# K of cache A two heads to a load, two K slots and two V slots, softmax and PV by head pair

## The chip, the cores and the metric

The kernel runs on one core of a Trainium2 chip. The core has a matrix engine (PE, with its weight loads shown as PEld), a vector engine (DVE), an activation engine (ACT), GpSimd (POOL) and SyncE (SP), which here issues nearly all loads. 16 DMA engines move the data between device memory and the core's own memory (SBUF, 128 partitions). The metric is the time of one execution on the device in microseconds (us).

## The reference

Two decode attentions stand side by side, A and B, each with its own inputs. Both have 32 query heads, 32 key and value heads of 16384 positions and 128 columns, and one query position. A attends to all positions, B to the last 4096.

```python
q = (x @ wq).reshape(B, Sq, Hq, Dh)              # x: 1 x 1 x 512, wq: 512 x 4096, bf16
k = k_cache ; v = v_cache                        # A: all 16384 positions
k = k_cache[:, :, Sk - W:, :]                    # B: W = 4096, v likewise
scores = jnp.einsum("bhqd,bhkd->bhqk", q, k) * (Dh ** -0.5)
p = _softmax(scores, axis=-1)
o = jnp.einsum("bhqk,bhkd->bhqd", p, v)
out = o.reshape(B, Sq, Hq * Dh) @ wo             # wo: 4096 x 512
return jnp.concatenate([a, b], axis=-1)
```

K and V are read once: 32 heads of 4 MiB each for A's K and for A's V, and as much as 8 heads each for B's.

## The kernel before

**Tiles.** The work is cut into 40 tiles of 4 MiB of K and 4 MiB of V (list `tiles`, L83). A tile of A is one head: each of the 128 partitions holds 128 consecutive positions, a row of 32 KB. A tile of B is four heads: partition 4i + h holds 128 positions of the window of head h. After every first of four A tiles stands a B tile.

**Buffers.** One ring of five slots of 32 KB per partition (`slot`, L62) holds K tiles, V tiles, the two wq and the two wo. Slots are handed out in the order of the loads: wq of A, K(0), wq of B, K(1), then V(t-1) and K(t+1) in turn. At the end come wo of B, V(38), V(39) and wo of A, the last in five pieces of 16, 8, 4, 2 and 2 rows (`wo_pieces`). All of these go through SP's queue, which works in order: a load whose slot isn't free holds up those behind it.

**One tile.** DVE multiplies K by the query row (`scores_prod`, L160), adds halves of the columns four times (`scores_tree`, L169), reduces the last eight columns (L173) and takes the maximum of each partition (`tile_max`, L180). PE transposes these maxima into one row (L182), DVE takes the maximum of the row (`max_all`, L187), one for A, four for B, which are spread to a row of 128 by a copy `Mr` (L194), and PE sends it back to all partitions (L198). ACT makes the bias (L207) and the exponentials with their sum (`soft`, L210); PE adds the sums over the partitions (L216). For B, ACT multiplies the exponentials by four masks into `pm` (L220), so that a matmul keeps four heads apart. PV is 32 matmuls of 128 x 512 (`pv`, L240), DVE inverts the sum (`recip`, L229), ACT scales the result (`evict`, L249), and four small matmuls turn it into a column of the output (`columns`, L259).

**Order.** The program is written out by hand (`manual_schedule`). In iteration t, DVE multiplies tile t before it takes the row maximum of tile t-1, then does the tree of tile t. PE's PV of tile t-1 runs beside that tree.

**End.** The last two tiles of A use V as weights and give a column directly (`pv_column`, L269). `permute_o` (L276 to L284) reorders the heads, `project_out_columns` (L294) multiplies by wo and `store_out` writes 512 columns. B's output is stored during the last iteration, A's last, as the pieces of its wo land.

Of the kernel before, what the change touches and what calls it, by code (L numbers as in the profile page):

```python
# [9 lines left out]
F32 = mybir.dt.float32  # L10
BF16 = mybir.dt.bfloat16
P = 128
# [5 lines left out]
NB = 5  # L18
# [8 lines left out]
def kernel(  # L27
# [22 lines left out]
    NI = P // 4  # L50
    assert WB == NI * CH

    singles = ctx.enter_context(tc.tile_pool(name="singles", bufs=1))
    ring = ctx.enter_context(tc.tile_pool(name="ring", bufs=NB))
    small = ctx.enter_context(tc.tile_pool(name="small", bufs=3))
    o_pool = ctx.enter_context(tc.tile_pool(name="o4", bufs=2))
# [5 lines left out]
    def slot(name):  # L62
        return ring.tile([P, CH, DH], BF16, tag="ring", name=name)
# [4 lines left out]
    ones_col = singles.tile([P, 1], F32, tag="ones_col")  # L68

    A, B = _Side(), _Side()  # L70
    for s, n, x, wq, wo in ((A, "A", A_x, A_wq, A_wo), (B, "B", B_x, B_wq, B_wo)):
        s.n, s.x, s.wq, s.wo = n, x, wq, wo
        s.xT = singles.tile([P, KC], BF16, tag=f"xT{n}", name=f"xT{n}")
        s.nh = 1 if n == "A" else 4
        s.xb = singles.tile([P, s.nh, KC, P], BF16, tag=f"xb{n}", name=f"xb{n}")
        s.q = singles.tile([P, HQ // s.nh, DH], BF16, tag=f"q{n}", name=f"q{n}")
        s.O = singles.tile([P, HQ], BF16, tag=f"O{n}", name=f"O{n}")
        s.Op = singles.tile([P, HQ], BF16, tag=f"Op{n}", name=f"Op{n}")
    mask4 = singles.tile([P, 4], F32, tag="mask4")
    mask16 = singles.tile([P, 4, 4], F32, tag="mask16")  # L80
    pick = singles.tile([HQ, 4, P], BF16, tag="pick")

    tiles = []  # L83
    for g in range(HQ // 4):
        tiles += [("A", 4 * g), ("B", g), ("A", 4 * g + 1), ("A", 4 * g + 2), ("A", 4 * g + 3)]
    NT = len(tiles)

    def load_kv(dst, cache, t):
        kind, h = tiles[t]
        if kind == "A":  # L90
            nc.sync.dma_start(out=dst[:, :, :], in_=cache[0][0, h, :, :].rearrange("(p l) d -> p l d", p=P))
        else:
            nc.sync.dma_start(
                out=dst[:, :, :].rearrange("p l d -> p (l d)"),
                in_=cache[1][0, 4 * h : 4 * h + 4, SkB - WB : SkB, :].rearrange(
                    "h (i l) d -> i h (l d)", l=CH
                ),
            )

    KSRC, VSRC = (A_k_cache, B_k_cache), (A_v_cache, B_v_cache)  # L100
    K, V = {}, {}

    def load_k(t):
        K[t] = slot("kt")
        load_kv(K[t], KSRC, t)

    def load_v(t):
        V[t] = slot("vt")
        load_kv(V[t], VSRC, t)

    def load_wq(s):
        s.wq_t = slot("wqt")
        nc.sync.dma_start(  # L113
            out=s.wq_t[:, :, :].rearrange("p a b -> p (a b)").rearrange("p (c f) -> p c f", c=KC),
            in_=s.wq.rearrange("(p c) f -> p c f", c=KC),
        )

    def load_wo(s, pieces):
        s.wo_t = slot("wot")
        dst = s.wo_t[:, :, :].rearrange("p a b -> p (a b)").rearrange("p (r f) -> p r f", r=HQ)  # L120
        src = s.wo.rearrange("(p r) f -> p r f", r=HQ)
        r = 0
        for n in pieces:
            nc.sync.dma_start(out=dst[:, r : r + n, :], in_=src[:, r : r + n, :])
            r += n

    def spread_x(s):
        if s.nh == 1:
            nc.vector.tensor_copy(s.xb[:, 0, :, :], s.xT[:, :].unsqueeze(2).broadcast_to([P, KC, P]))
        else:  # L130
            nc.vector.memset(s.xb[:, :, :, :], 0.0)
            for j in range(s.nh):
                nc.vector.tensor_copy(
                    s.xb[:, j, :, :].rearrange("p c (i h) -> p c i h", h=s.nh)[:, :, :, j],
                    s.xT[:, :].unsqueeze(2).broadcast_to([P, KC, P // s.nh]),
                )

    def project_q(s):
# [3 lines left out]
        G = HQ // s.nh  # L142
        for g in range(0, G, 4):
# [10 lines left out]
    sc, pt, mx, sm, osb = {}, {}, {}, {}, {}  # L154

    def scores_prod(t):
        kind, h = tiles[t]
        k = K[t]
        q = (A if kind == "A" else B).q
        nc.vector.tensor_tensor(  # L160
            out=k[:, :, :], in0=k[:, :, :], in1=q[:, h : h + 1, :].broadcast_to([P, CH, DH]), op=ALU.mult
        )

    def scores_tree(t):
        k = K[t]
        sc[t] = small.tile([P, CH], F32, tag="sc", name="sc")
        w = DH // 2
        while w >= 8:
            nc.vector.tensor_tensor(  # L169
                out=k[:, :, 0:w], in0=k[:, :, 0:w], in1=k[:, :, w : 2 * w], op=ALU.add  # L170
            )
            w //= 2
        nc.vector.tensor_reduce(out=sc[t][:, :], in_=k[:, :, 0:8], axis=AX.X, op=ALU.add)  # L173

    def nq_of(t):
        return 1 if tiles[t][0] == "A" else 4

    def tile_max(t):
        m = small.tile([P, 1], F32, tag="m", name="m")
        nc.vector.tensor_reduce(out=m[:, :], in_=sc[t][:, :], axis=AX.X, op=ALU.max)  # L180
        sm[t] = ps_m.tile([P, 512], F32, tag="sm", name="sm")
        nc.tensor.transpose(sm[t][0:1, 0:P], m[:, :], identf[:, :])  # L182

    def max_all(t):
        nq = nq_of(t)
        M = small.tile([1, 4], F32, tag="M", name="M")
        nc.vector.tensor_reduce(  # L187
            out=M[:, 0:nq], in_=sm[t][0:1, 0:P].rearrange("o (i q) -> o q i", q=nq), axis=AX.X, op=ALU.max
        )
        if nq == 1:  # L190
            row = M[:, 0:1].broadcast_to([1, P])
        else:
            Mr = small.tile([1, P], F32, tag="Mr", name="Mr")
            nc.vector.tensor_copy(  # L194
                Mr[:, :].rearrange("o (i q) -> o i q", q=nq), M[:, :].unsqueeze(1).broadcast_to([1, P // nq, nq])
            )
            row = Mr[:, :]
        nc.tensor.matmul(sm[t][:, 128:129], lhsT=row, rhs=one_f[:, :], start=True, stop=True)  # L198

    def rows_of(t):  # L200
        if t >= NT - 2:
            return P
        return 4 if tiles[t][0] == "A" else 16

    def soft(t):
        bias = small.tile([P, 1], F32, tag="bias", name="bias")
        nc.scalar.activation(out=bias[:, :], in_=sm[t][:, 128:129], func=ACT.Copy, scale=-inv)  # L207
        pt[t] = small.tile([P, CH], BF16, tag="p", name="p")
        cs = small.tile([P, 1], F32, tag="cs", name="cs")
        nc.scalar.activation(  # L210
            out=pt[t][:, :], in_=sc[t][:, :], func=ACT.Exp, scale=inv, bias=bias[:, :], accum_out=cs[:, :]
        )
        ns = rows_of(t)
        lhsT = cs[:, :].broadcast_to([P, ns]) if ns != 16 else mask16[:, :, :].rearrange("p a b -> p (a b)")
        rhs = ones_col[:, :] if ns != 16 else cs[:, :]
        nc.tensor.matmul(sm[t][0:ns, 136:137], lhsT=lhsT, rhs=rhs, start=True, stop=True)  # L216
        if ns == 16:
            pm = o_pool.tile([P, CH // 4, 4, 4], BF16, tag="pm", name="pm")
            for j in range(4):
                nc.scalar.activation(  # L220
                    out=pm[:, :, j, :], in_=pt[t][:, :].rearrange("p (i c) -> p i c", c=4),
                    func=ACT.Copy, scale=mask4[:, j : j + 1],
                )
            pt[t] = pm

    def recip(t):
        ns = rows_of(t)
        r = small.tile([P, 1], F32, tag="r", name="r")
        nc.vector.reciprocal(r[0:ns, :], sm[t][0:ns, 136:137])  # L229
        sm[t, "r"] = r  # L230

    def pv(t):
        n = rows_of(t)
        o = ps_o.tile([16, 512], F32, tag="o", name="o")
        for i in range(CH // 4):
            if n == 4:
                lhsT = pt[t][:, 4 * i : 4 * i + 4]
            else:
                lhsT = pt[t][:, i, :, :].rearrange("p a b -> p (a b)")
            nc.tensor.matmul(  # L240
                o[0:n, :], lhsT=lhsT, rhs=V[t][:, 4 * i : 4 * i + 4, :],
                start=(i == 0), stop=(i == CH // 4 - 1),
            )
        sm[t, "o"] = o

    def evict(t):
        n = rows_of(t)
        osb[t] = o_pool.tile([16, 512], F32, tag="o4", name="o4")
        nc.scalar.activation(  # L249
            out=osb[t][0:n, :], in_=sm[t, "o"][0:n, :], func=ACT.Copy, scale=sm[t, "r"][0:n, 0:1]  # L250
        )

    def columns(t):
        kind, h = tiles[t]
        n, nq = rows_of(t), nq_of(t)
        oc = sm[t][:, 140 : 140 + nq]
        sel = identf[0:n, 0:n].rearrange("k (h c) -> k c h", c=4)
        for j in range(4):
            nc.tensor.matmul(  # L259
                oc, lhsT=osb[t][0:n, j * P : (j + 1) * P], rhs=sel[:, j, :], start=(j == 0), stop=(j == 3)  # L260
            )
        s = A if kind == "A" else B
# [153 lines left out]
```

## Time and profile before

| | |
|---|---|
| time, median of 3 runs (lowest to highest) | 829.92 us (829.76 to 830.18) |
| the profiled execution: its own time | 830.12 us |
| its span in the profile | 828.3 us |
| mean clock granted to PE | 0.72 of full |
| read from device memory | 352.32 MB, mean 426 GB/s of traffic |
| busy: DVE, PE, PEld, ACT | 764.5, 461.9, 203.9, 77.8 us |
| a K load, a V load, from issue to landing (median) | 38.6, 29.7 us |

How to read the profile: engines are shown with the time in which an instruction ran on them. A group of instructions is named by its line (L160 is line 160 of the kernel), its engine and operation, and the tiles that it writes and reads. `out<-in 128x512 bf16` gives partitions, elements and type; `x32` is a count. In the timeline a row begins with the start and the duration in us, and in brackets stands the idle time before it, with what ended it. In the list of waits a row gives the waiting engine, what it waited for, the total in us, how often and the longest. The page's slices are 40 equal parts of the span. The DMA queue q1 is SP's.

### The profile page before, as it was taken

How to read it: one execution, taken by the hardware profiler on the slowest of the kernel's cores; microseconds unless marked ns; L12 is line 12 of the kernel's file. 1: busy time of each engine (PE TensorE's matmuls, PEld its weight loads, DVE VectorE, ACT ScalarE, POOL GpSimd, SP SyncE). 2: the span in 40 equal slices, each digit the busy share in tenths (PEclk: the TensorE clock that was granted, in tenths of full speed). 3: DMA queues.
4: the chain of work that ended last, by engine and by line, in shares of the span. 5: the costliest groups of instructions: out<-in, count | busy, mean ns of one | idle time of the engine just before them, and what ended most of it. 6: DMA issues, size and time to landing. Idle time of an engine off the chain costs nothing.

```text
span 828.3 us, 5565 instructions
## 1 busy us (share of the span) xinstructions
PE 461.9 (56%) x2308; PEld 203.9 (25%) x2308; DVE 764.5 (92%) x387; ACT 77.8 (9%) x247; POOL 0.7 (0%) x6
## 2 busy tenths in 40 slices
PE   3544655555555656556655555555565565555645
PEld 1212222222222222222222222222222222222234
DVE  1899999999999999999999999999999999999980
ACT  1101100010001100010100100001100100011110
POOL 0000000000000000000000000000000000000000
PEclk9776876776776677777777677666667787776755
DMA  9999999999999999999999999999999999999996
GB/s 380 430 430 430 430 430 430 435 435 434 431 432 432 428 434 432 428 430 431 432 430 430 432 430 434 432 428 432 429 434 432 432 430 434 430 430 435 431 430 260
DMA packets 13000, 352.68 MB, mean 426 GB/s; under 512 B 1712, under 2 KB 1712, under 8 KB 2096
## 3 DMA queue, kind: packets, MB, share of 16 engines
q1 hardware_dynamic: 12680, 352.33, 99.0%
q8 instruction: 18, 0.29, 0.1%
q10 hardware_dynamic: 296, 0.00, 0.0%
q14 instruction: 6, 0.05, 0.0%
HBM read 352.32 MB, written 0.00 MB: 425 GB/s over the span
## 4 chain that ended last, share of the span: by engine, by line
DMA 68%; DVE 18%; PE 12%; ACT 1%; issue 0%; SPq 0%; DVEq 0%
DMA kt<-in_A_k_cache_dram 47%; DMA kt<-in_B_k_cache_dram 14%; DVE kt L160 14%; PE o L240 11%; DMA wot<-in_A_wo_dram 4%; DMA wot<-in_B_wo_dram 4%; DVE kt L169 3%; PE sm L198 1%; ACT p L210 1%; DVE sc L173 0%; ACT pm L220 0%; DVE M L187 0%; ACT bias L207 0%; PE sm L216 0%; SPq L113 0%
## 5 line engine op out<-in xcount | busy, mean ns | idle before, releaser
L169 DVE TENSOR_TENSOR kt<-kt 128x8192 bf16<-128x8192 bf16 (+3 forms) x160 | 344.5, 2153 | 4.2
L160 DVE TENSOR_TENSOR kt<-kt,qA 128x16384 bf16<-128x16384 bf16 x32 | 278.2, 8693 | 14.3 <-DMA kt<-in_A_k_cache_dram 13.8
L240 PE MATMUL o<-vt,p 128*4 128x512 bf16 x960 | 276.7, 460 | 0.6 <-DMA vt<-in_A_v_cache_dram 0.6
L240 PEld LDWEIGHTS <-p 128*4 128x4 bf16 x960 | 92.7, 98 | 170.1 <-issue 94.2
L198 PE MATMUL sm<-one_f,M 1*128 1x1 f32 x64 | 18.6, 357 | 205.9 <-DVE M L187 205.9
L240 PE MATMUL o<-vt,pm 128*16 128x512 bf16 x256 | 74.2, 462 | 8.8 <-ACT pm L220 8.8
L160 DVE TENSOR_TENSOR kt<-kt,qB 128x16384 bf16<-128x16384 bf16 x8 | 69.5, 8693 | 2.6 <-DMA kt<-in_B_k_cache_dram 2.6
L198 PEld LDWEIGHTS sm<-one_f,M 1*128 1x128 f32 x64 | 15.9, 306 | 209.0 <-DVE M L187 209.0
L249 ACT ACTIVATE o<-o,r 4x512 f32<-4x512 f32 (+1 forms) x38 | 25.8, 678 | 356.7 <-PE o L240 330.5
L259 PE MATMUL sm<-identf,o 4*128 4x1 f32 (+1 forms) x304 | 39.8, 248 | 19.1 <-ACT o L249 18.9
L173 DVE TENSOR_REDUCE sc<-kt 128x128 f32<-128x1024 bf16 x40 | 48.8, 1220 | 1.4
L259 PEld LDWEIGHTS sm<-identf,o 4*128 4x128 f32 (+1 forms) x304 | 36.6, 186 | 26.5 <-ACT o L249 26.5
L240 PEld LDWEIGHTS <-pm 128*16 128x16 bf16 x256 | 26.3, 105 | 53.4 <-issue 24.6
L198 PE MATMUL sm<-one_f,Mr 1*128 1x1 f32 x16 | 4.7, 357 | 59.8 <-DVE Mr L194 59.8
L207 ACT ACTIVATE bias<-sm 128x1 f32<-128x1 f32 x40 | 6.9, 172 | 286.7 <-PE sm L198 286.7
L216 PE MATMUL sm<-ones_col,cs 128*4 128x1 f32 (+1 forms) x64 | 6.9, 177 | 25.2 <-ACT p L210 25.2
L198 PEld LDWEIGHTS sm<-one_f,Mr 1*128 1x128 f32 x16 | 4.0, 306 | 60.4 <-DVE Mr L194 60.4
L306 DVE TENSOR_REDUCE cols<-out_cols 128x4 f32<-128x20 f32 x1 | 0.2, 179 | 18.9 <-PE out_cols L294 18.9
L148 PE MATMUL qp<-wqt,xbA 128*128 128x512 bf16 x32 | 9.6, 475 | 13.6 <-DMA wqt<-in_A_wq_dram 13.6
L210 ACT ACTIVATE p<-sc,bias 128x128 bf16<-128x128 f32 x40 | 16.1, 402 | 1.3
L182 PE MATMUL sm<-identf,m 128*1 128x128 f32 x40 | 10.9, 272 | 6.3 <-DVE m L180 6.2
L148 PE MATMUL qp<-wqt,xbB 128*128 128x512 bf16 x32 | 8.4, 428 | 9.9 <-DMA wqt<-in_B_wq_dram 9.9
(54 smaller groups left out, 116.6 us busy)
## 6 DMA issues: line engine op xcount, KB each, us to landing
kt<-in_A_k_cache_dram SPq DMA_DIRECT2D x32, 4096.0 KB, 38.6
vt<-in_A_v_cache_dram SPq DMA_DIRECT2D x32, 4096.0 KB, 29.7
kt<-in_B_k_cache_dram SPq DMA_DIRECT2D x8, 4096.0 KB, 38.7
vt<-in_B_v_cache_dram SPq DMA_DIRECT2D x8, 4096.0 KB, 29.7
wqt<-in_A_wq_dram SPq DMA_DIRECT2D x1, 4096.0 KB, 12.8
wqt<-in_B_wq_dram SPq DMA_DIRECT2D x1, 4096.0 KB
wot<-in_B_wo_dram SPq DMA_DIRECT2D x1, 4096.0 KB, 29.4
wot<-in_A_wo_dram SPq DMA_DIRECT2D x1, 2048.0 KB, 33.5
```

The costliest lines, as they stand in the source:

```text
L148: nc.tensor.matmul(qp[:, :, :], lhsT=s.xb[:, j, c, :], rhs=wq[:, c, j, g : g + 4, :], start=(k == 0), stop=(k == n - 1),)
L160: nc.vector.tensor_tensor(out=k[:, :, :], in0=k[:, :, :], in1=q[:, h : h + 1, :].broadcast_to([P, CH, DH]), op=ALU.mult)
L169: nc.vector.tensor_tensor(out=k[:, :, 0:w], in0=k[:, :, 0:w], in1=k[:, :, w : 2 * w], op=ALU.add)
L173: nc.vector.tensor_reduce(out=sc[t][:, :], in_=k[:, :, 0:8], axis=AX.X, op=ALU.add)
L182: nc.tensor.transpose(sm[t][0:1, 0:P], m[:, :], identf[:, :])
L198: nc.tensor.matmul(sm[t][:, 128:129], lhsT=row, rhs=one_f[:, :], start=True, stop=True)
L207: nc.scalar.activation(out=bias[:, :], in_=sm[t][:, 128:129], func=ACT.Copy, scale=-inv)
L210: nc.scalar.activation(out=pt[t][:, :], in_=sc[t][:, :], func=ACT.Exp, scale=inv, bias=bias[:, :], accum_out=cs[:, :])
L216: nc.tensor.matmul(sm[t][0:ns, 136:137], lhsT=lhsT, rhs=rhs, start=True, stop=True)
L240: nc.tensor.matmul(o[0:n, :], lhsT=lhsT, rhs=V[t][:, 4 * i : 4 * i + 4, :], start=(i == 0), stop=(i == CH // 4 - 1),)
L249: nc.scalar.activation(out=osb[t][0:n, :], in_=sm[t, "o"][0:n, :], func=ACT.Copy, scale=sm[t, "r"][0:n, 0:1])
L259: nc.tensor.matmul(oc, lhsT=osb[t][0:n, j * P : (j + 1) * P], rhs=sel[:, j, :], start=(j == 0), stop=(j == 3))
```

## The change

The loads of A's K take two heads at once: partition 64h + i of an 8 MiB tile holds 256 positions of head h of the pair, a row of 64 KB. There are two slots of 64 KB per partition for K and two of 32 KB for V in place of five of 32 KB. A step T is a pair of tiles: a pair of A's heads, or two B tiles of four heads. V of a step comes in two loads of 4 MiB: for an A pair each takes 128 of the 256 positions of every partition, so it is read in rows of 32 KB that stand 64 KB apart. B's tiles keep their layout. The steps of B are the first, 7, 13 and the last, 19.

DVE's product, tree and reduction run on half a step at a time (u = 0, 1), 4 MiB as before. For an A pair there is one softmax for both heads, over 256 columns per partition, with two masks into `pm`; the sum of PV over both halves goes into one accumulator. For B there is a softmax for every half. PV of an A pair is two times 32 matmuls with 8 rows of output instead of 4: `pv(T-2, 1)` and `pv(T-1, 0)` both stand in the first half of step T. The last half step uses V as weights, for four heads of B; A's output is stored first, B's last, as the pieces of its wo land. The scratch for B's spread x takes a K slot at the start.

SP's order in step T is V(T-1, 0), K(T+1), V(T-1, 1). In step 19 it is V(18, 0), V(18, 1), V(19, 0), wo of A, V(19, 1), wo of B in five pieces.

The core of the diff:

```diff
-    ring = ctx.enter_context(tc.tile_pool(name="ring", bufs=NB))
+    kring = ctx.enter_context(tc.tile_pool(name="kring", bufs=2))
+    vring = ctx.enter_context(tc.tile_pool(name="vring", bufs=2))
...
+    def kslot(name):
+        return kring.tile([P, 2 * CH, DH], BF16, tag="kring", name=name)
+
+    def vslot(name):
+        return vring.tile([P, CH, DH], BF16, tag="vring", name=name)
...
+    for T in range(HQ // 2 + HQ // 8):
+        if T in (0, 7, 13, 19):
+            steps.append((B, nb))
+            nb += 1
+        else:
+            steps.append((A, na))
+            na += 1
...
+    def b_window(cache, g):
+        return cache[0, 4 * g : 4 * g + 4, SkB - WB : SkB, :].rearrange("h (i l) d -> i h (l d)", l=CH)
+
+    def a_pair(cache, g):
+        return cache[0, 2 * g : 2 * g + 2, :, :].rearrange("h (i l) d -> (h i) l d", l=2 * CH)
...
+    def load_k(T, u=None):
+        s, g = steps[T]
+        if s is A:
             nc.sync.dma_start(
...
+                out=K[T][:, :, :].rearrange("p l d -> p (l d)"),
+                in_=a_pair(A_k_cache, g).rearrange("p l d -> p (l d)"),
+            )
+        else:
+            for v in (0, 1) if u is None else (u,):
+                nc.sync.dma_start(
+                    out=K[T][:, v * CH : (v + 1) * CH, :].rearrange("p l d -> p (l d)"),
+                    in_=b_window(B_k_cache, 2 * g + v),
+                )
+
+    def load_v(T, u):
+        s, g = steps[T]
+        V[T, u] = vslot("vt")
+        if s is A:
+            src = a_pair(A_v_cache, g)[:, u * CH : (u + 1) * CH, :].rearrange("p l d -> p (l d)")
+        else:
+            src = b_window(B_v_cache, 2 * g + u)
+        nc.sync.dma_start(out=V[T, u][:, :, :].rearrange("p l d -> p (l d)"), in_=src)
...
+    def unit_max(un):
         m = small.tile([P, 1], F32, tag="m", name="m")
...
+        nc.vector.tensor_reduce(out=m[:, :], in_=un.sc[:, 0 : un.n], axis=AX.X, op=ALU.max)
+        un.sm = ps_m.tile([P, 512], F32, tag="sm", name="sm")
+        nc.tensor.transpose(un.sm[0:1, 0:P], m[:, :], identf[:, :])
...
+        for j in range(s.nh):
+            nc.scalar.activation(
+                out=un.pm[:, :, j, :], in_=p[:, 0 : un.n].rearrange("p (i c) -> p i c", c=4),
+                func=ACT.Copy, scale=s.mask[:, j : j + 1],
+            )
...
+    def pv(T, u):
+        s = steps[T][0]
+        un = units[T, u if s is B else 0]
+        first, final = (True, True) if s is B else (u == 0, u == 1)
+        if first:
+            un.o = ps_o.tile([16, 512], F32, tag="o", name="o")
+        i0 = u * CH // 4 if s is A else 0
+        for i in range(CH // 4):
+            nc.tensor.matmul(
+                un.o[0 : un.rows, :],
+                lhsT=un.pm[:, i0 + i, :, :].rearrange("p a b -> p (a b)"),
+                rhs=V[T, u][:, 4 * i : 4 * i + 4, :],
+                start=(first and i == 0),
+                stop=(final and i == CH // 4 - 1),
             )
...
+        for x in range(2 * NT):
+            T, u = divmod(x, 2)
+            if u == 0 and T >= 1:
+                load_v(T - 1, 0)
+                if T + 1 < NT:
+                    new_k(T + 1)
+                    load_k(T + 1)
+            if x == 2 * NT - 1:
+                load_v(T, 0)
+                W = kslot("wot")
+                load_wo(A, W, 0, (HQ,))
+            columns()
+            scores_prod(T, u)
+            if done is not None:
+                max_all(done)
+                soft(done)
+            if u == 0 and T >= 1:
+                if T >= 2:
+                    pv(T - 2, 1)
+                load_v(T - 1, 1)
+                pv(T - 1, 0)
+            if x == 2 * NT - 1:
+                pv(T - 1, 1)
+                load_v(T, 1)
+                load_wo(B, W, 1, wo_pieces)
+            nxt = scores_tree(T, u)
+            if done is not None:
+                recip(done)
+            evict()
+            done = nxt
+            if done is not None:
+                unit_max(done)
```

## The prediction

> **What bounds the kernel now.** I read the page first, slices and chain before groups, then the waits of all engines and of SP's queue, then the timeline of the last 90 us. From the page:
>
> ```profile
> span 828.3 us, 5565 instructions
> ...
> PE 461.9 (56%) x2308; PEld 203.9 (25%) x2308; DVE 764.5 (92%) x387; ACT 77.8 (9%) x247; POOL 0.7 (0%) x6
> ...
> GB/s 380 430 430 430 430 430 430 435 435 434 431 432 432 428 434 432 428 430 431 432 430 430 432 430 434 432 428 432 429 434 432 432 430 434 430 430 435 431 430 260
> ...
> q1 hardware_dynamic: 12680, 352.33, 99.0%
> ...
> DMA 68%; DVE 18%; PE 12%; ACT 1%; issue 0%; SPq 0%; DVEq 0%
> ```
>
> The DMA engines are 99% occupied and move 428 to 435 GB/s in every slice but the first and the last. The kernel is bound by 84 loads of 4 MiB: at 432 GB/s one takes 4.194/0.432 = 9.71 us, and 84 take 815.6. DVE at 92% is close behind. The waits say how close:
>
> ```profile
> DVE kt L160 <- DMA kt<-in_A_k_cache_dram: 13.8, 25, 3.0
> DVE kt L160 <- DMA kt<-in_B_k_cache_dram: 2.6, 8, 0.4
> ```
>
> DVE waits for K only 16.4 us in 40 tiles. The issuing queue is the third clock:
>
> ```profile
> SPq L91 <- DVE m L180: 544.0, 30, 20.7
> SPq L93 <- DVE m L180: 149.2, 8, 19.2
> ```
>
> SP spends its time waiting for ring slots, yet the median K load lands 38.6 us after its issue (part 6 of the page), four loads' worth: slots come free two loads ahead of need. No idle DMA is visible for a better order to recover. From the timeline:
>
> ```profile
> 745.30 8.69 DVE L160 TENSOR_TENSOR kt<-kt,qA 128x16384 bf16<-128x16384 bf16 x1 [0.39 <-DMA kt<-in_A_k_cache_dram]
> ...
> 754.22 0.21 DVE L194 COPY Mr<-M 1x128 f32<-1x128 f32 x1
> ...
> 757.16 9.89 PE L240 MATMUL o<-vt,pm 128*16 128x512 bf16 x32 [1.09 <-ACT pm L220]
> ...
> 764.74 8.69 DVE L160 TENSOR_TENSOR kt<-kt,qA 128x16384 bf16<-128x16384 bf16 x1
> ...
> 784.09 8.69 DVE L160 TENSOR_TENSOR kt<-kt,qA 128x16384 bf16<-128x16384 bf16 x1 [0.26 <-DMA kt<-in_A_k_cache_dram]
> ```
>
> A step with B's four-row softmax takes 764.74 - 745.30 = 19.44 us of DVE, one with A's 784.09 - 764.74 - 0.26 + 0.1 of usual spacing = 19.19. The wait at 784.09 is for the last K, the 80th load. Loads 81 to 84 and the last wo piece (first used at 824.72) follow 40.6 us behind, and 3.6 us after that the span ends. The time before is 830.12 for this execution (span 828.3) and 829.92 in the median, 0.2 apart, so a difference of ends carries over to the median.
>
> **The change, part by part.**
>
> *Bytes.* The same 84 x 4 MiB. A's K goes in 16 loads of 8 MiB with 64 KB rows. In the trace's DMA records a packet of 32 KB takes 1.215 us and one of 16 KB 0.612, so 16 KB cost 0.603 and a packet about 9 ns more. If 64 KB go as one packet, each of 16 DMA engines saves 8 x 9 ns a pair, 1.15 us in 16 pairs; if rows are cut at 32 KB, nothing. Fewer DMAs save nothing else: landings follow each other at 9.71 us, the packets' own time. *DMA: Bandwidth & Descriptors* (Anatomy of one DMA) in the Trainium skill puts about 2.0 us of fixed cost on a DMA, measured on another issue path; by that, 16 fewer would save up to 32 us.
>
> *Row pitch.* A's V is read as 32 KB rows 64 KB apart, A's K as an unbroken 8 MiB. B's tiles already take neighbouring partitions from heads 4 MiB apart, and their stretches run at the same 429 to 432 GB/s. I take no loss. The same page (Latency and other measured facts) speaks against the change here: row pitches of large powers of two lose rate, 3% at 512 KiB and half at 4 MiB. B's rows contradict it at 4 MiB; by its 3%, 32 V loads would cost 9.3 us.
>
> *DVE.* The product (8.69), tree (8.72) and reduction (1.22) are unchanged per 4 MiB. Per A pair the change takes away one maximum over partitions (0.1 on DVE's path), one reciprocal (0.04) and one row maximum (0.3), adds the Mr copy (0.2 to 0.25), and lengthens the remaining row maximum from 128 to 256 columns (0 to 0.29 more, from 0.286; I take 0.13). A pair is 2 x 19.19 - 0.44 + 0.25 + 0.13 = 38.3; bounds 38.1 to 38.5. A B pair is 2 x 19.44 = 38.9. The loads of a pair take 38.85. So DVE and DMA run nearly level, as before.
>
> *ACT and PE.* Two mask multiplications of 256 columns per pair (0.390 for 128, so about 0.5 each) lie beside DVE's tree. PE's 32 matmuls per 4 MiB of V stay. They come as 64 in a row once per pair: pv(T-2,1), then pv(T-1,0). The trace has no such burst. Alone, 32 take 8.6 to 9.9: the first 13 start 0.427 apart, the rest 0.21. So the first half takes 9.5 and the second between 32 x 0.21 = 6.8 and 9.5; I take 6.8, since the spacing doesn't grow again within a burst. *TensorE: Matmul & The Clock Gate* (Part 1) says the clock doubles after some 3.4 us of activity and falls back after an idle window of that length; the rows show about 5.5 us, and the rule too gives 6.8.
>
> *Queue, in the body.* SP now waits for pv(T-2,1) before it issues V(T-1,1), and V(T,0) and K(T+2) stand behind that wait. From the step's start: product 8.69; maximum and Mr 0.45; broadcast on PE 0.6; bias, exponential over 256 columns, its accumulator and the row-sum matmul 1.15; together 10.9. Then 9.5 of PV: the slot is free at 20.4. Meanwhile V(T-1,0) and the 8 MiB K(T+1) have kept the DMA engines busy for 29.1 us from about the step's start. Covered by 8 us; cost nothing. K(T+1) needs its slot at the step's start and has V(T-1,0)'s 9.7 us as cover. Two B steps (7 and 13) have a maximum whose transpose queues behind both PVs: 10.9 + 9.5 + 6.8 + 0.3 = 27.5, against DVE's arrival at 19.44 + 8.69 = 28.1. No wait at the chosen PV, 2 us each at the slow one.
>
> *Queue, at the end.* In step 19 there is no K(20). V(18,0), the 79th load, is alone in the queue, and V(18,1), the 80th, is not issued until pv(17,1) ends; V(19,0), wo of A, V(19,1) and wo of B stand behind it. The cover of 19.4 us is gone.
>
> - DVE starts at 23.4 as before, since K still lands second. The first B pair ends at 42.8 + 19.44 = 62.3 (42.8 is where DVE starts its second tile now, its load being fourth in both; halves of a slot are waited for apart, as the pieces of wo are now at 822.16 and 823.43). Then 16 x 38.3 + 2 x 38.9 = 690.6: step 19 starts at 752.9 by DVE alone.
> - By DMA: K(18) is loads 72 and 73. Load 76 starts the product of 745.30, so load 73 ends at 745.0 - 29.1 = 715.9, or 714.8 with larger packets. Plus 0.3 and step 18's 38.3: 753.4 to 754.5.
> - Both agree; I take 754.2. Plus 20.4 is 774.6, when SP may issue. The kernel's first load takes from 0.74 to 2.17 from issue to its first byte, 1.4; so 776.1.
> - Load 79 ends at 784.1 - 9.7 = 774.4. The engines idle 1.7 us.
> - Load 80 takes 9.71 plus a restart. The first load landed at 13.62, 1.7 later than 2.17 + 9.71; bounds 0 and 1.7, I take 0.7, nearer zero because three other first loads were issued within the same 2 us there. It is usable at 776.1 + 9.7 + 0.7 + 0.2 = 786.7, against 784.1.
>
> The four loads behind it are as many and as cut as now, and the end is the same chain of projection, transpose and store. pv(18,0) ends at 774.6 + 6.8 = 781.4, before load 80 does, and pv(18,1) at about 796.5, before wo of A (about 806) does, so no second gap. Sum: 786.7 - 784.1 = 2.6 later; 829.9 + 2.6 = 832.5.
>
> **Rivals.**
>
> - *The gap doesn't open.* If DVE's pair is 38.1 and 64 KB packets are real, step 19 starts at 752.5 to 753; with no restart cost load 80 is usable within 1.4 us of its old time. 830.1, from 829.2 to 831.5. For it: the two clocks differ by under 0.2%. Against: it needs the favourable end of three terms.
> - *Slow PV.* If the second PV stays at 9.5, two B steps lose 2 us each, and a first PV up to 10.5 adds 1: 754.2 + 2 to 4 + 20.4 to 21.4. 836, to 838.
> - *DMA slowed by the new rows.* 0.5% of A's K and V, 2/3 of 650 us: 2 to 3 us more than the forecast, 835.
> - *Faster, by quicker K rows.* It decides once load 80 lands before 782.4, so step 19 must start by 749.9 and K(18) land by 711.3, 4.6 earlier than now. Seventeen pairs of K, 330 us, would have to run 1.4% faster, and DVE's pair to take 38.1. The packets explain 1.15 us. 827.5.
> - *It doesn't do what it says:* rows cut into 32 KB packets. That moves the DMA line by 1.1 us and is inside the forecast's range.
>
> **How the numbers follow.** Forecast 0.55, its own range 830.6 to 834.5; no gap 0.21; slow PV 0.11; slower rows 0.07; faster 0.06. No change means within 0.2%, 1.7 us, about what a measurement of this kernel can tell. About 0.06 of the forecast's chance and nearly all of the second case lie there: same 0.26, faster 0.07, slower 0.67. The range from 829.4 to 836.5 leaves out the faster case, the worst of slow PV and small parts of the rest.
>
> **What would show it.** Right: no "9" missing in the DMA slices until a dip around 774; SP's longest late wait ends with PE's PV; the product of step 19 starts near 754; V(18,1) lands near 787; 64 matmuls in a row with 16.3 us between first and last. Wrong: slices of the body above 434 or below 429 GB/s; DVE waiting for the transposed maximum in B steps; waits for K of several us in A steps; a step 19 that starts before 751 or after 757.

## The result, and the profile after

The changed kernel takes 831.33 us in the median of 14 runs (830.11 to 832.50), the kernel before 829.86 in 14 runs beside it (829.58 to 830.18): 1.47 us slower, a ratio of 1.0018 with a 95% interval of 1.0010 to 1.0026. The profiled execution took 831.32, with a span of 829.5.

The page of the changed kernel, lines that answer to those shown of before: span, busy time by engine, what the DMA engines moved in each of 40 slices, SP's queue, and the chain that ended last.

```profile
span 829.5 us, 4817 instructions
...
PE 395.2 (48%) x2012; PEld 172.7 (21%) x2012; DVE 761.0 (92%) x356; ACT 67.8 (8%) x196; POOL 0.7 (0%) x6
...
GB/s 379 430 430 437 433 458 411 453 408 432 435 427 430 437 455 411 450 412 448 416 444 417 440 425 431 450 416 450 416 441 420 444 417 443 425 433 433 331 431 305
...
q1 hardware_dynamic: 10376, 352.33, 98.7%
...
DVE 79%; DMA 17%; PE 2%; issue 1%; SPq 0%; ACT 0%; DVEq 0%; ACTq 0%
```

One slice stands out, the 38th with 331 GB/s (767 to 788 us). The swing of the others around 432 is a matter of counting (see the section on why the prediction was right); the dip is real. The windows around it, first of the changed kernel, then of the one before (stretch, length, busy time of each engine with its instructions, granted clock, DMA share, GB/s):

```profile
760.00:767.00 7.00, 3.94 (x12) 1.54 (x13) 6.93 (x5) 1.68 (x5) 0.00 (x0) 0.50 0.97 417
767.00:774.00 7.00, 7.00 (x30) 2.63 (x29) 6.83 (x7) 0.68 (x1) 0.00 (x0) 0.87 0.45 190
774.00:781.00 7.00, 7.00 (x36) 3.10 (x35) 7.00 (x2) 0.00 (x0) 0.00 (x0) 1.00 0.99 393
```

```profile
767.00:774.00 7.00, 1.64 (x12) 1.36 (x11) 7.00 (x3) 0.84 (x2) 0.00 (x0) 0.70 1.01 435
```

Before, the DMA engines were full in these 7 us; now they are 45% full, so on average each stands idle for 3.9 us. What they wait for stands in SP's own waits between 773 and 774 us and in the timeline of the changed kernel:

```profile
SPq L131 <- PE o L275: 9.9, 1, 9.9
```

```profile
752.99 8.68 DVE L194 TENSOR_TENSOR kt<-kt,qB 128x16384 bf16<-128x16384 bf16 x1
...
763.70 16.50 PE L275 MATMUL o<-vt,pm 128*8 128x512 bf16 x64
...
773.31 0.33 SPq L131 DMA_DIRECT2D vt<-in_A_v_cache_dram  x1
...
785.39 8.98 PE L275 MATMUL o<-vt,pm 128*8 128x512 bf16 x32 [2.48 <-DMA vt<-in_A_v_cache_dram]
...
825.78 0.38 PE L345 MATMUL out_cols<-OpB,wot 128*128 128x1 bf16 x8 [0.27 <-DMA wot<-in_B_wo_dram]
```

Step 19 begins at 752.99; `pv(17, 1)` and `pv(18, 0)` are the 64 matmuls from 763.70; when the first 32 are done, SP issues V(18,1), the 80th load, at 773.31, and PE can use it at 785.39. In the kernel before the 80th load was used at 784.09. From there on both kernels run alike: the last wo piece is used at 825.78 against 824.72, and the span ends 3.7 us later against 3.6.

### The profile page after: what moved, and what is told of

Its sections match the earlier page's. It is cut to its first block, busy times and chain, and to the rows that moved or that the text cites. A ratio compares the mean times of both kernels' runs of the same rounds, so it can differ in the third digit from the quotient of the medians.

```text
span 829.5 us, 4817 instructions
## 1 busy us (share of the span) xinstructions
PE 395.2 (48%) x2012; PEld 172.7 (21%) x2012; DVE 761.0 (92%) x356; ACT 67.8 (8%) x196; POOL 0.7 (0%) x6
## 3 DMA queue, kind: packets, MB, share of 16 engines
q1 hardware_dynamic: 10376, 352.33, 98.7%
## 4 chain that ended last, share of the span: by engine, by line
DVE 79%; DMA 17%; PE 2%; issue 1%; SPq 0%; ACT 0%; DVEq 0%; ACTq 0%
DVE kt L194 36%; DVE kt L201 35%; DMA kt<-in_A_k_cache_dram 10%; DVE sc L207 5%; DMA wot<-in_B_wo_dram 3%; DMA xTA<-in_A_x_dram 3%; PE o L275 2%; DMA vt<-in_A_v_cache_dram 1%; DVE m L212 1%; DVE Mr L223 1%; DVE M L219 0%; SPq L145 0%; DVE r L263 0%; ACT p L234 0%; PE sm L226 0%
## 5 line engine op out<-in xcount | busy, mean ns | idle before, releaser
L275 PE MATMUL o<-vt,pm 128*8 128x512 bf16 (+1 forms) x1248 | 316.3, 420 | 2.5 <-DMA vt<-in_A_v_cache_dram 2.5
L275 PEld LDWEIGHTS <-pm 128*8 128x8 bf16 (+1 forms) x1248 | 116.2, 94 | 192.5 <-issue 65.1
L226 PE MATMUL sm<-one_f,Mr 1*128 1x1 f32 x48 | 13.1, 340 | 176.7 <-DVE Mr L223 176.7
L226 PEld LDWEIGHTS sm<-one_f,Mr 1*128 1x128 f32 x48 | 11.1, 285 | 183.1 <-DVE Mr L223 183.1
L291 ACT ACTIVATE o<-o,r 8x512 f32<-8x512 f32 (+1 forms) x23 | 15.6, 678 | 176.5 <-PE o L275 176.5
L306 PE MATMUL oc<-identf,o 8*128 8x2 f32 (+1 forms) x184 | 25.1, 254 | 3.7 <-ACT o L291 3.7
L306 PEld LDWEIGHTS oc<-identf,o 8*128 8x128 f32 (+1 forms) x184 | 23.1, 193 | 12.0 <-issue 6.5
L172 PE MATMUL qp<-wqt,scratch 128*128 128x512 bf16 x32 | 9.1, 455 | 13.8 <-DVE scratch L161 13.8
L253 ACT ACTIVATE pm<-p,maskA 128x256 bf16<-128x256 bf16 x32 | 14.5, 500 | 0.5
L234 ACT ACTIVATE p<-sc,bias 128x256 bf16<-128x256 f32 (+1 forms) x24 | 11.3, 472 | 0.8
L253 ACT ACTIVATE pm<-p,maskB 128x128 bf16<-128x128 bf16 x32 | 10.2, 389 | 0.2
```

Source lines behind the costliest of these rows:

```text
L172: nc.tensor.matmul(qp[:, :, :], lhsT=s.xb[:, j, c, :], rhs=wq[:, c, j, g : g + 4, :], start=(k == 0), stop=(k == n - 1),)
L226: nc.tensor.matmul(un.sm[:, 128:129], lhsT=Mr[:, :], rhs=one_f[:, :], start=True, stop=True)
L234: nc.scalar.activation(out=p[:, 0 : un.n], in_=un.sc[:, 0 : un.n], func=ACT.Exp, scale=inv, bias=bias[:, :], accum_out=cs[:, :],)
L253: nc.scalar.activation(out=un.pm[:, :, j, :], in_=p[:, 0 : un.n].rearrange("p (i c) -> p i c", c=4), func=ACT.Copy, scale=s.mask[:, j : j ...
L275: nc.tensor.matmul(un.o[0 : un.rows, :], lhsT=un.pm[:, i0 + i, :, :].rearrange("p a b -> p (a b)"), rhs=V[T, u][:, 4 * i : 4 * i + 4, :], ...
L291: nc.scalar.activation(out=un.osb[0 : un.rows, :], in_=un.o[0 : un.rows, :], func=ACT.Copy, scale=un.r[0 : un.rows, 0:1],)
```

## The experiments

Three explanations compete. Theory 1: the end moves with the landing of the 80th load, and this waits for `pv(17, 1)` to free a V slot. Theory 2: the end is set by DVE's step after step, as the chain's 79% suggests. Theory 3: the idle time only lets late DMA engines catch up, so closing it would gain little.

**V(18,1) into a slot that is free (e1_slot).** The K slot of step 18 is empty when step 19 begins. V(18,1) goes there, and the loads behind it are spread over what is left.

```diff
+                else:
+                    W = kslot("wot")
+                    load_v(T - 1, 1, W[:, 0:CH, :])
             if x == 2 * NT - 1:
                 load_v(T, 0)
-                W = kslot("wot")
-                load_wo(A, W, 0, (HQ,))
+                load_wo(A, vslot("wot"), 0, (HQ,))
+                load_v(T, 1, W[:, CH : 2 * CH, :])
...
-                load_v(T, 1)
-                load_wo(B, W, 1, wo_pieces)
+                load_wo(B, W, 0, wo_pieces)
```

> V(18,1) is loaded into the K slot that step 18 has left, so it no longer waits for pv(17,1); V(19,0) and wo of A take the two V slots, V(19,1) and wo of B the halves of that K slot. Theory 1 (the whole loss is the wait before the 80th load): the 80th load follows the 79th without a pause, is usable at about 782.9 instead of 785.4, and the end comes 2.0 to 2.6 us earlier: 828.7 to 829.3, below the kernel before. Theory 2 (DVE's chain of step after step, 79% of the chain that ended last, sets the end): within 0.5 us of 831.3. Theory 3 (the restart only lets lagging DMA engines catch up, so closing it gives the lag back): a gain under 1 us, 830.3 to 831.3.

Measured: 828.14 us (11 runs, 827.75 to 828.96), a ratio of 0.9979 to the kernel before, 0.9970 to 0.9988; 3.2 us below the changed kernel. Its timeline and its window:

```profile
752.51 0.33 SPq L131 DMA_DIRECT2D wot<-in_A_v_cache_dram  x1
...
763.56 8.51 PE L275 MATMUL o<-vt,pm 128*8 128x512 bf16 x32
...
782.72 8.75 PE L275 MATMUL o<-wot,pm 128*8 128x512 bf16 x32
```

```profile
767.00:774.00 7.00, 6.06 (x29) 2.37 (x28) 6.83 (x7) 0.68 (x1) 0.00 (x0) 1.00 1.00 428
```

SP issues the load 20.8 us earlier, the engines stay full, and PE uses the load at 782.72, 2.7 earlier. Step 19 begins when it did (752.86 against 752.99), so DVE's chain up to there is unchanged while the end came 3.2 us earlier: theory 2 is out, and so is theory 3, which allowed less than 1 us. This version beats both kernels.

A part of theory 3 does show at the load itself: the engines had idled 3.9 us each, and the load came only 2.7 earlier. By the landing records of the two traces, the 16 engines finish V(18,1) within 0.5 us of each other after the gap (784.87 to 785.35) and 3.3 us apart without it (779.41 to 782.68), so late engines do catch up in the gap. But nothing is given back in the end: the last piece of wo lands at 821.85 instead of 825.73, the whole 3.9 us earlier.

**A lighter DVE (e5_light).** The other end of theory 2:

```diff
-        while w >= 8:
+        while w >= 16:
```

> The last of the four additions of each tree (8 columns, 0.69 us on DVE) is left out, so the scores lack columns 8 to 15; DVE has 28 us less to do over the run. Theory 1: the loads and then the wait for pv(17,1) set the end; V(17,1) lands at 763.2 whatever DVE does, so pv(17,1) can start at most 0.5 us earlier, and DVE waits for K instead: 830.7 to 831.4. Theory 2 (DVE's chain sets the end): at least 3 us less, 828.3 or below.

Measured: 830.86 us (11 runs), 0.5 below the changed kernel. Its page and its waits:

```profile
DMA 49%; DVE 45%; PE 5%; issue 0%; SPq 0%; ACT 0%; DVEq 0%
```

```profile
DVE kt L194 <- DMA kt<-in_A_k_cache_dram: 23.9, 12, 3.2
DVE kt L194 <- DMA kt<-in_B_k_cache_dram: 5.4, 2, 4.4
```

```profile
763.09 9.12 PE L275 MATMUL o<-vt,pm 128*8 128x512 bf16 x32 [1.05 <-DMA vt<-in_A_v_cache_dram]
...
772.24 0.33 SPq L131 DMA_DIRECT2D vt<-in_A_v_cache_dram  x1
```

DVE is busy for 26.5 us less (734.5 against 761.0), and its waits for K grow by 26.3, from 3.0 to 29.3. The same 80th load is issued at 772.24, after a `pv(17, 1)` that now starts as its V lands. DVE and the DMA engines take nearly the same time for a step (38.1 us a pair in the changed kernel against four loads of 9.7). The chain's 79% DVE had shown only that DVE was the later of the two at most steps; the share didn't tell what a faster DVE brings.

**A's K in two loads of 32 KB rows (e2_rows32).**

```diff
-            nc.sync.dma_start(
-                out=K[T][:, :, :].rearrange("p l d -> p (l d)"),
-                in_=a_pair(A_k_cache, g).rearrange("p l d -> p (l d)"),
-            )
+            for v in (0, 1):
+                nc.sync.dma_start(
+                    out=K[T][:, v * CH : (v + 1) * CH, :].rearrange("p l d -> p (l d)"),
+                    in_=a_pair(A_k_cache, g)[:, v * CH : (v + 1) * CH, :].rearrange("p l d -> p (l d)"),
+                )
```

> A's K is loaded in two halves of 32 KB rows per pair, all else as in the changed kernel. Theory 1: packets of 32 KB only, so each DMA engine needs 1.15 us more over the run; V(17,1) lands about 1.1 later, pv(17,1) starts 0.5 to 1.1 later, and the end moves by as much: 831.8 to 832.5. Theory 2 (DVE's chain): no change or a small gain, since a product can start on half a pair: 830.8 to 831.4. If long rows were bad for the transfers, 830 or less.

Measured: 832.12 us (8 runs, 831.62 to 832.78), 0.8 above the changed kernel. Products could start on half a pair and step 19 began earlier, at 749.95, yet `pv(17, 1)` did not:

```profile
764.85 16.75 PE L276 MATMUL o<-vt,pm 128*8 128x512 bf16 x64 [4.05 <-DMA vt<-in_A_v_cache_dram]
...
774.46 0.33 SPq L132 DMA_DIRECT2D vt<-in_A_v_cache_dram  x1
```

It waits 4.05 us for V(17,1), which lands 1.4 us later by the landing records (764.81 against 763.40). Each DMA engine has two packets of 32 KB in place of one of 64 KB, 128 times, at 10 ns more each time: an estimated 1.3 of it. The 80th load is issued 1.15 later and the end follows, by 0.8 in the median and 1.2 in the profiled execution.

**PE kept busy ahead of `pv(17, 1)` (e4_warm).** 24 matmuls without a use stand in step 19 between the first product's start and its maximum.

```diff
+            if x == 2 * NT - 2:
+                wm = ps_t.tile([8, 512], F32, tag="tp", name="warm")
+                for i in range(24):
+                    nc.tensor.matmul(wm[:, :], lhsT=ident[:, 0:8], rhs=A.q[:, 0:4, :], start=(i == 0), stop=(i == 23))
             if done is not None:
                 max_all(done)
```

> 24 matmuls of 8 x 512 whose result is not used run on PE during the first product of step 19, ahead of pv(17,1). Theory 1: pv(17,1) runs at the full clock, 6.9 us instead of 9.5, SP issues V(18,1) at about 770.8 instead of 773.3, its first byte comes at about 772.3, when the slowest DMA engine is not yet done with the 79th load; the end comes 1.5 to 2.5 us earlier: 828.8 to 829.8. Theory 2 (DVE's chain): 831.3 within 0.5. Theory 3 (lag given back): a gain under 1 us.

Measured: 830.36 us (11 runs), 1.0 below the changed kernel, less than expected. The timeline and the windows (granted clock third from the end) show why:

```profile
753.41 7.41 PE L416 MATMUL warm<-qA,ident 128*8 128x512 bf16 x24
...
763.39 8.76 PE L275 MATMUL o<-vt,pm 128*8 128x512 bf16 x32
...
772.18 0.33 SPq L131 DMA_DIRECT2D vt<-in_A_v_cache_dram  x1
```

```profile
757.00:761.00 4.00, 3.83 (x16) 1.27 (x14) 4.00 (x1) 0.00 (x0) 0.00 (x0) 0.92 1.03 442
761.00:765.00 4.00, 2.04 (x11) 1.02 (x12) 3.97 (x4) 1.68 (x5) 0.00 (x0) 0.93 0.99 426
765.00:769.00 4.00, 4.00 (x14) 1.29 (x13) 3.93 (x3) 0.00 (x0) 0.00 (x0) 0.64 1.02 438
```

The clock was full when `pv(17, 1)` began at 763.39, and then fell back within it: the last extra matmul had ended at 760.8, and in the 2.6 us between PE ran only four small matmuls. The PV took 8.76 us instead of 9.58, not 6.9. Even this 0.8 can't be put down to the extra matmuls: in e1_slot, without them, the same PV took 8.51. In the Trainium skill, *TensorE: Matmul & The Clock Gate* (Part 1) has the clock judged in free-running windows of about 3.4 us, which fits a fall that comes after the pause; by the rows here, a pause of 2.6 us was enough for it. As a test of theory 1 the run still serves: issue 1.13 us earlier, end 1.0 earlier.

The five kernels side by side, times in us; issue and use are counted from the span's start, and the last two columns go by the time of the same, profiled execution:

| kernel | 80th load issued | used by PE | time of this execution | time less use |
|---|---|---|---|---|
| changed | 773.31 | 785.39 | 831.32 | 45.9 |
| e2_rows32 | 774.46 | 786.52 | 832.52 | 46.0 |
| e4_warm | 772.18 | 784.21 | 830.34 | 46.1 |
| e5_light | 772.24 | 784.39 | 830.38 | 46.0 |
| e1_slot | 752.51 | 782.72 | 828.96 | 46.2 |

Before, the 80th load was used at 784.09 in an execution of 830.12: 46.0. The four edits spread the use of this load over 3.8 us, and the end follows within 0.3 each time. That is theory 1. In e1_slot the agreement is in part chance: its last load landed 3.9 us earlier than in the changed kernel, but PE was late at the end of this execution.

**What remains at the end of the better version (e6_order, e7_order_rows32).** In the profiled execution of e1_slot, PE is late at the end. The chain, in order of time:

```profile
807.76 3.50 PE out_cols L345 x126
811.26 1.01 issue
812.27 0.21 PE out_cols L345 x2
...
816.40 2.06 issue
818.46 0.23 PE ocol L317 x3
```

e6_order loads wo of A before V(19,0) and moves three calls ahead of `pv(19, 0)` (the edit is shown against e1_slot):

```diff
-                load_v(T, 0)
                 load_wo(A, vslot("wot"), 0, (HQ,))
+                load_v(T, 0)
...
         recip(done)
+        permute_o(A)
+        project_out_columns(A, (HQ,))
+        store_out(A)
         pv(NT - 1, 0)
         evict()
         columns()
-        permute_o(A)
-        project_out_columns(A, (HQ,))
-        store_out(A)
```

> As the kernel with V(18,1) in the free K slot, but wo of A is loaded before V(19,0), and A's output is computed and stored before pv(19,0) instead of after it. There PE reached its last 128 matmuls at 820.1 us, with all of wo of B landed at 821.6, and the span ended 5.6 us after the landing instead of 3.9. Theory (the last stretch there is PE's, held up by A's output and by two pauses of 1.0 and 2.1 us for which the profile shows no releaser): with 4 us of PE's work moved ahead of the last V load, the end follows the last piece of wo again and comes 1.0 to 1.8 us earlier: 826.4 to 827.2. Rival (the transfers alone set the end): 828.1 within 0.4.

Measured: 828.22 us (11 runs, 827.51 to 828.47), no gain over 828.14: the rival came true. The profiled execution of e6_order does wait for the last piece of wo, with a span 0.9 shorter:

```profile
822.51 0.37 PE L345 MATMUL out_cols<-OpB,wot 128*128 128x1 bf16 x8 [0.25 <-DMA wot<-in_B_wo_dram]
```

But the profiled execution of e1_slot was the slowest of its 11 runs (828.96). So the two pauses probably belonged to that execution and not to the kernel; no other execution of e1_slot was profiled, so this is not shown.

e7_order_rows32 adds the halved K loads of e2_rows32 to it.

> The same with A's K in two halves of 32 KB rows per pair. If the 16 packets of 9 ns that each pair saves (8 per DMA engine with long rows against 16, 1.15 us per engine over the run) reach the end once no wait stands before it: 0.8 to 1.3 us more than the same kernel with 64 KB rows, 827.4 to 828.2. Rival (the long rows are worth nothing because DVE sets the pace): the same within 0.4.

Measured: 829.21 us (11 runs, 828.71 to 829.85), 1.0 more than e6_order on the same chip. With no wait before them the long rows are worth about what their packets save. This run is still 0.7 below the kernel before (ratio 0.9990, 0.9981 to 0.9999); where this rest comes from was not tested. So the gap hid a gain: without it, as in e1_slot, the change is worth 1.8 us.

## Why the prediction was right

The mechanism forecast is the one found: SP's wait for `pv(17, 1)`, harmless through the body, uncovered in step 19. The time lay inside the range, 1.2 us below the forecast, and the move was 1.5 us instead of 2.6. Point by point:

- *Packets.* The DMA records show 2048 packets of 64 KB at 2.420 us and the 32 KB ones at 1.215 as before: 10 ns saved each, against 9. SP's queue went from 12680 to 10376 packets. As forecast the saving did not reach the end by itself; e2_rows32 shows that without it the end is 0.8 later, since V(17,1) would land later. Sixteen more loads cost that. By the 2.0 us of fixed cost in the Trainium skill (*DMA: Bandwidth & Descriptors*, Anatomy of one DMA), which the page gives for another issue path, they would have cost an estimated 32; in this full queue no such cost shows. Where the queue had run dry, 773.31 to 785.39 is 12.1 us for a load of 9.7: 2.4 above it, against 2.3 in the sum (1.4 + 0.7 + 0.2).
- *Row pitch.* 32 KB packets, A's V among them, take what they took, 1.215 us. The Trainium skill (*DMA: Bandwidth & Descriptors*, Latency and other measured facts) gives its figures on large powers of two for pitches from 512 KiB on, from copies within device memory; here neither the 64 KB pitch of A's V nor the 4 MiB between B's neighbouring rows shows a loss.
- *DVE.* Products of equal halves follow at 444.07, 482.20 and 520.34: 38.14 us a pair, with 38.3 forecast and 38.1 as the lower bound.
- *PV.* 64 matmuls in 16.50 us, 9.58 for the first 32; forecast 16.3 and 9.5. In the B steps 7 and 13 DVE doesn't wait for the transposed maximum. It does once, for 2.9 us at 794.62, because that transpose stands behind the late `pv(18, 1)`; this comes of the gap and not of a slow PV. Slow PV is out.
- *The step that was off* is the start of step 19: 752.99 against 754.2. The working had 752.9 by DVE and 753.4 to 754.5 by DMA, and I took a value near the top. K(18) could be used at 714.85 (forecast 715.1) and step 18 took 38.14. From there to the issue it is 20.32 (forecast 20.4). These 1.2 us are nearly the whole difference: the load was used at 785.39, not 786.7.
- *From issue to use* the sum of 12.1 came out by luck, with two errors that cancel: the first byte came 1.0 us after the issue (at 774.28; 1.4 in the sum), and the load took 11.1 from there to its landing, 1.4 above 9.7 (0.7 in the sum). The idle time of 1.7 us is right for the time in which no engine works (772.65 to 774.28); the 3.9 on average come about because the engines finish the 79th load at different times, from 769.15 on.
- *A test that was wrongly set.* Slices above 434 or below 429 GB/s should have spoken against me; the body has 408 to 458. Over a pair the rate is 432 to 433, and e2_rows32, with packets of 32 KB, shows 428 to 437 again. The swing is a matter of counting: the row books a packet of 64 KB, which lasts 2.4 us, a ninth of a slice, wholly in the slice in which it starts. With the bytes of the same records spread over each packet's time, all body slices of the changed kernel hold 430 to 434, and the dip remains (340).
- *The rivals.* The gap opened, by 55% of 7 us; slower rows and quicker rows were not seen.

What stays open: the changed kernel's runs spread over 2.4 us, those of before over 0.6. The experiments say nothing of why.

## What to carry to other kernels

A slot's wait is covered by what stands before it in the queue, so ask of the last step, where the next big load no longer comes, what covers it then. Where two engines take nearly the same time for a step, the share of the chain is no measure of what an engine is worth; take work off it, or look where the loads run dry. A buffer that falls free at the end (here a K slot of 64 KB) can take the load that would wait.

## What was not expected of the hardware

PE's granted clock (mean of 4 us) fell from 0.93 to 0.64 within a PV of 32 matmuls after a pause of 2.6 us ahead of it (e4_warm), so 24 matmuls that ended before that pause did not keep the clock up for the burst. And the 16 DMA engines drift apart in a long stream: in the kernel before they land the first load of SP's queue within 0.6 us of each other (12.98 to 13.57) and the 80th within 3.7 us (780.42 to 784.07); a gap in the queue brings them together again (0.5 us in the changed kernel).
